# Attention with normalised queries and keys, then a SiLU feed-forward: a score unit moved in the late visits, two small writes moved to ScalarE, and another order and bank behind the last visit

## The chip, the cores and the metric

The kernel runs on one core of a Trainium2 chip. The metric is the device time of one execution in microseconds (us), and less is better. The engines are TensorE (PE in the profile; its weight loads are PEld), VectorE (DVE), ScalarE (ACT), GpSimd (POOL) and SyncE (SP, which issues most of the transfers). They run side by side, and each takes its own instructions in program order and waits for the others by semaphores.

## The reference

All inputs are 32-bit floats. Attention has 8 batches, 12 heads, 448 positions and 64 columns to a head; the feed-forward takes 3584 rows of 768 columns through 2048 hidden columns.

```python
def rmsnorm(x, g):
    rms = np.sqrt(np.mean(x * x, axis=-1, keepdims=True) + 1e-06)
    return x / rms * g
q_n, k_n = rmsnorm(q, g_q), rmsnorm(k, g_k)
scores = np.matmul(q_n, k_n.transpose(0, 1, 3, 2)) / np.sqrt(64)
attn = np.exp(scores - np.max(scores, axis=-1, keepdims=True))
attn = attn / (np.sum(attn, axis=-1, keepdims=True) + 1e-09)
x = np.matmul(attn, v).transpose(0, 2, 1, 3).reshape(8 * 448, 768)
h = x @ w_in
out = (h / (1 + np.exp(-h))) @ w_out
```

## The kernel before

**Visits.** The 96 heads are taken four at a time, as two pairs, in 24 *visits*: `visit(c)` for c from 0 to 23, and a last `visit(24)` that only finishes visit 23. Six visits are a group of two batches (`GROUP`). From visit 12 on (`LATE`) queries and keys are loaded in quarters and transposed by VectorE instead of TensorE. These are the late visits.

**What a visit does.** TensorE works in *units* of four 64 x 64 matmuls, which are written into one place of PSUM. A score unit (`scores`, matmuls on L709) fills one of two buffers named `sc`, and two exponentials on ScalarE (L714) read it into SBUF; the next unit but one in `sc` waits until they have. A value unit (`weigh`, L746) multiplies exponentials with rows of V, and adds into two banks, `av0` and `av1`, one for each pair of heads. A visit has seven score units and seven value units. They are written out by hand in one order, which is the order on TensorE. The last three value units of visit c - 1 (`weigh(c - 1, LEFT)`, `weigh(c - 1, LEFT - 1, 0)` and `weigh(c - 1, LEFT - 1, 1)`) lie in visit c. Then `divide(c - 1, sums)` on VectorE (L804, two instructions) reads both banks, multiplies by the reciprocal sums and writes columns of `x`. The first value unit of visit c, `weigh(c, 0, 1)`, writes the same two banks again: its first half waits for the divide of `av0`, its second half for that of `av1`.

**The one-column writes.** Where consecutive value units change the order of the array's halves, `turn` (L722) writes one unused column of bank `av1`, which waits for the matmuls into that bank and holds the next ones back. ScalarE or VectorE does it:

```python
turn(1, nc.scalar.copy if c <= GROUP else nc.vector.tensor_copy)
```

**Between visits.** `between(c)` makes the sums of exponentials and their reciprocals for visit c, prepares the next visits, and fills TensorE with the first layer of the feed-forward for the group before: products in Strassen's manner, seven for each block, from `x` and from `sums_x` (L882), in banks named `mm`. `scale(c + 2)` puts one small product in an `sc` buffer, which VectorE reads (L682). At the end of a group `sum_x` forms the differences of the columns of `x` that products 3 to 7 use: four VectorE instructions (L837) for each of three column indices. Index 0 is done in `between`, behind the last product that reads the old sums; indices 1 and 2 follow in the next visit, behind its divides.

**After the last visit.** When `visit(24)` is done, the six banks of `sc`, `av0` and `av1` go to a pool named `ps_alone`, and two more stay as `mm`. `bank` deals products out in turns of four, one to `mm` and three to `ps_alone`; `turns["next"]` says where it starts. The last group's first layer follows (L882), and then the second layer (L1226, and L1189 for most of it). Weight rounding and sums go beside it on VectorE, ScalarE and GpSimd.

Of the kernel before, what the change touches and what calls it, by code (L numbers as in the profile page):

```python
# [532 lines left out]
def bounded(  # L533
# [4 lines left out]
    HW, HF = z.NW // 2, z.NF // 2  # L538
# [5 lines left out]
    NC, loads, place, norm, spare, ones, first, squares = (  # L544
        own[name] for name in ("NC", "loads", "place", "norm", "spare", "ones", "first", "squares")
    )
    GROUP, LATE = z.NPAIR, z.LATE
# [55 lines left out]
    def weights(c, j):  # L603

        return other if j == 0 and c < GROUP and c % 2 else e[j]
# [4 lines left out]
    def x_of(c, i):  # L610
        b, cp = divmod(c, z.NPAIR // 2)
        return xT(b, 2 * cp + i)
# [87 lines left out]
    def scores(c, j, i=None):  # L700


        two = ps.tile([P, 2, BANK], F32, name="sc", bufs=2)
        for half in range(2):
            pair = half if j == LEFT else i
            keys = kT[:, ds((z.KA, z.KB)[0 if j == LEFT else i] + j * P, P)]
            for h in range(2):
                rows = ds(h * D, D)
                nc.tensor.matmul(  # L709
                    two[ds(half * D, D), h, 0:S], keys[rows, ts(half, D)], qT[rows, pair, :],  # L710
                    start=True, stop=True,
                )
        for h in range(2):
            nc.scalar.activation(  # L714
                eleft[:, h] if j == LEFT else weights(c, j)[:, i, h], two[:, h, 0:S], AF.Exp,
                scale=norm.column(c, i, h, j),
            )

    def turn(step, copy):

        if step != weighed["step"]:
            copy(banks[1][:, S : S + 1], minus_half)  # L722
# [78 lines left out]
    def divide(c, source):  # L801
        for i in range(2):
            x = x_of(c, i)
            nc.vector.tensor_tensor(  # L804
                out=x, in0=x if source is None else source[i], in1=r[i], op=ALU.mult
            )

    def normalise(c):


        def piece(name, i):
            t = scratch[i if c < GROUP + 2 else 0]
            source = raw_of(c) if c < GROUP else q_of(c)
            if name == "q":
                norm.squares_q(c, source, t, i)
            else:
                norm.squares_k(c, place["k0" if c >= LATE else f"k{c % 2}"], t, i)
            if name == "q" and c < GROUP:
                norm.root(c, name, i)
                norm.scale(c, source, q_of(c), i, nc.gpsimd)  # L820
                if i == 1 and c + 2 < GROUP:
                    load_q(c + 2)
            elif i == 1:
                norm.root(c, name)
                if name == "q":
                    for m in range(2):
                        norm.scale(c, source, q_of(c), m, nc.gpsimd)
                elif LATE <= c < NC - 1:
                    loads["k"](c + 1)

        if c >= NC:
            return []
        return [lambda a=a: piece(*a) for a in (("q", 0), ("q", 1), ("k", 0), ("k", 1))]
# [26 lines left out]
    turns = dict(next=0)  # L860
# [92 lines left out]
    def sum_x(group, c):  # L953
        right_sums(*quarters(group, c), *sums_of_x(c))
# [355 lines left out]
    def begin(work, columns, parts):  # L1310
        finish()
        filler.update(work=work, due=0.0, share=columns / parts)
# [31 lines left out]
    def finish():  # L1344
        run(filler["work"])
# [19 lines left out]
    def weights_in_visit(c):  # L1365
        for step in visits.get(c, ""):
            step_of[step]()
        if c in sums_visits:
            for step in range(4):
                sum_w_in(sums_visits[c], step)  # L1370

    def last_two(c):
        return [c // GROUP * 2 - 2, c // GROUP * 2 - 1]

    def visit(c):

        beside = normalise(c + 1) if c <= GROUP else []
        if c < NC:
            scores(c, 0, 0)
        run_all(beside[0:1])  # L1380
        if c > 0:
            weigh(c - 1, LEFT)
            weigh(c - 1, LEFT - 1, 0)
            turn(1, nc.scalar.copy if c <= GROUP else nc.vector.tensor_copy)
        if c < NC:
            scores(c, 0, 1)
        if c == 0:
            run_all(beside[1:2])
        if c > 0:
            weigh(c - 1, LEFT - 1, 1)  # L1390
            if c - 1 < EARLY:
                for i in range(2):
                    nc.vector.tensor_copy(x_of(c - 1, i), sums[i])
                run_all(beside[1:2])
                if inverting:
                    if c > 1:
                        divide(c - 2, None)
                    run_all(inverting)
                    inverting.clear()
            else:  # L1400
                divide(c - 1, sums)
                run_all(beside[1:2])
                if c < NC and c % GROUP == 0:
                    for i in range(0 if c == GROUP else 1, HW):
                        sum_x(last_two(c), i)
                weights_in_visit(c)
            if c + 1 < NC:
                loads["vrest"](c + 1)
        if c == NC:
            return  # L1410
        scores(c, 1, 0)
        scores(c, 1, 1)
        if c < GROUP:
            run_all(beside[2:3])
        weigh(c, 0, 1)
        scores(c, 2, 0)
        weigh(c, 1, 1)
        turn(0, nc.scalar.copy)
        if c < GROUP:
            run_all(beside[3:4])  # L1420
        scores(c, 2, 1)
        weigh(c, 0, 0)
        run_all(add(c, 1))
        weigh(c, 1, 0)
        scores(c, LEFT)
        if c + 1 < NC:
            loads["v"](c + 1)

    def run_all(work):
        for piece in work:  # L1430
            piece()

    def between(c):

        def transposes_and_sums():
            summing = sum_up(c)
            if c < GROUP:
                next(summing)
            if c < LATE - 1:
                transpose_k(c + 1)  # L1440
            reciprocals = next(summing)
            if LATE - 1 <= c < NC - 1:
                reciprocals += [lambda: flip(c + 1, "k"), gain]
            if GROUP // 2 <= c <= EARLY:
                divide(c - 1, None)
            return reciprocals

        if c < LATE - 1:
            transpose_q(c + 1)
        elif c < NC - 1:  # L1450
            flip(c + 1, "q")
        if c < GROUP // 2:
            inverting.extend(transposes_and_sums())
        elif c == GROUP - 1:
            run_all(transposes_and_sums())
        if c >= GROUP and c % GROUP == 0:
            fetched = range(AHEAD) if c == GROUP else ()
            columns = products - 2 * HW * S * len(fetched)
            work = halves_in(last_two(c), range(HF), plain_in, dict(begun), fetched)
            begin(work, columns, 2 * GROUP)  # L1460
            begun.clear()
        late = add(c, LEFT - 1) + add(c, LEFT) if c >= GROUP else []
        further = normalise(c + 2) if c >= GROUP - 1 else []
        fill(late + weights_in(c, 0) + further[2:])
        prompt = transposes_and_sums() if GROUP // 2 <= c != GROUP - 1 else []
        if c == GROUP // 2:
            begin(make_ahead([0, 1]), AHEAD * 2 * HW * S, GROUP - 1)
        if c >= LATE - 2:
            if c == LATE - 2:
                prompt.append(pair_up)  # L1470
            queries = prompt[3:] + [lambda: sum_squares(c + 2)]
            fill(weights_in(c, 1), prompt[:3] + [lambda: run_all(queries)])
        else:
            fill(weights_in(c, 1) + (further[:2] if c >= GROUP else []), prompt)
        if c % GROUP == GROUP - 1:
            finish()
            if c == GROUP - 1:
                begun[0] = fetch_ahead([0, 1], 0)
            else:
                sum_x([c // GROUP * 2, c // GROUP * 2 + 1], 0)  # L1480
        if c >= LATE - 2:
            scale(c + 2)
        if GROUP <= c < NC - 1:

            nc.scalar.activation(first, minus_half, AF.Exp)
        if c == NC - 1:
            while rounder.load():
                pass
# [12 lines left out]
    ps_alone = ctx.enter_context(  # L1501
        tc.tile_pool(name="ps_alone", bufs=6, space=bass.MemoryType.PSUM)
    )
    turns["next"] = 1
    group = [z.B - 2, z.B - 1]
    for i in (1, HW - 1):
        sum_x(group, i)
    for m in range(2):
        rows = [staged() for _ in range(2)]
# [215 lines left out]
```

## Time and profile before

| | |
|---|---|
| median of 3 runs | 1331.43 us (1331.42 to 1336.38) |
| profiled execution | 1333.6 us |
| its span in the profile | 1331.8 us |
| TensorE busy | 1301.7 us, 98% |
| VectorE busy | 942.2 us, 71% |
| ScalarE busy | 506.6 us, 38% |
| GpSimd busy | 363.8 us, 27% |
| late visits begin (first score) | visit 12 at 334.09 us, visit 18 at 538.39 us, visit 23 at 708.15 us |
| last visit and start of the last group's products | 742.7 to 748.3 us |

A span is the time from the first to the last instruction of the profiled execution. A row of a timeline gives start, length, engine, line, operation, what it writes and reads, and how many instructions of that kind were merged; in brackets how long the engine stood idle ahead of it, and what ended that. The end of a matmul in such rows is modelled, so the starts are the firmer numbers. A row of waits gives the engine and line that waited, who was waited for, the total in us, how often, and the longest.

### The profile page before, as it was taken

How to read it: one execution, taken by the hardware profiler on the slowest of the kernel's cores; microseconds unless marked ns; L12 is line 12 of the kernel's file. 1: busy time of each engine (PE TensorE's matmuls, PEld its weight loads, DVE VectorE, ACT ScalarE, POOL GpSimd, SP SyncE). 2: the span in 40 equal slices, each digit the busy share in tenths (PEclk: the TensorE clock that was granted, in tenths of full speed). 3: DMA queues.
4: the chain of work that ended last, by engine and by line, in shares of the span. 5: the costliest groups of instructions: out<-in, count | busy, mean ns of one | idle time of the engine just before them, and what ended most of it. 6: DMA issues, size and time to landing. Idle time of an engine off the chain costs nothing.

```text
span 1331.8 us, 19793 instructions
## 1 busy us (share of the span) xinstructions
PE 1301.7 (98%) x7189; PEld 833.1 (63%) x7189; DVE 942.2 (71%) x1623; ACT 506.6 (38%) x890; POOL 363.8 (27%) x229
## 2 busy tenths in 40 slices
PE   8998999999999999999999999999999999999998
PEld 4333444444444444444444455557999999999998
DVE  5787777785755555854554586688978787878785
ACT  7876556655454554455545244410001000001000
POOL 5765534344333433433330154410000000000000
PEclk9999999999999999999999999999999999999999
DMA  8564436333444444444321257522323232332311
GB/s 231 149 167 134 119 98 168 103 89 94 95 94 115 98 93 117 94 94 115 88 66 62 97 179 249 171 74 76 99 76 99 76 105 83 97 105 71 127 48 39
DMA packets 249487, 144.94 MB, mean 109 GB/s; under 512 B 184292, under 2 KB 233316, under 8 KB 249380
## 3 DMA queue, kind: packets, MB, share of 16 engines
q1 hardware_dynamic: 248816, 142.60, 38.0%
q8 instruction: 59, 0.97, 0.3%
q0 software_dynamic: 256, 0.79, 0.2%
q14 instruction: 48, 0.39, 0.1%
q10 hardware_dynamic: 308, 0.20, 0.1%
HBM read 93.98 MB, written 41.29 MB: 102 GB/s over the span
## 4 chain that ended last, share of the span: by engine, by line
PE 84%; DVE 7%; ACT 3%; issue 3%; DMA 2%; POOL 1%; SPq 0%; ACTq 0%; DVEq 0%; POOLq 0%
PE mm L882 26%; PE alone L1189 22%; PE av L746 8%; PE sc L709 7%; PE mm L1189 7%; PE alone L882 7%; PE alone L1226 2%; DVE work L760 1%; PE sc L780 1%; DVE work L789 1%; DVE sums_x L837 1%; DMA work<-work 1%; PE mm L1226 1%; PE sc L644 1%; PE sc L626 0%
## 5 line engine op out<-in xcount | busy, mean ns | idle before, releaser
L882 PE MATMUL mm<-x,W 128*128 128x448 f32 x636 | 256.7, 546 | 6.1 <-DVE parts L840 2.3
L714 ACT ACTIVATE work<-sc,rms 128x448 f32<-128x448 f32 x324 | 184.7, 633 | 81.0 <-PE sc L709 64.9
L882 PEld LDWEIGHTS mm<-x,W 128*128 128x128 f32 x636 | 116.7, 190 | 138.0 <-issue 109.0
L882 PE MATMUL mm<-sums_x,W 128*128 128x448 f32 x456 | 183.7, 543 | 1.6 <-DVE parts L840 1.6
L709 PE MATMUL sc<-work 64*64 64x448 f32 x1344 | 168.2, 549 | 2.6 <-ACT work L714 1.4
L746 PE MATMUL av<-work,rows 64*64 64x448 f32 x1296 | 156.6, 543 | 6.3 <-ACT av L722 1.8
L760 DVE TENSOR_TENSOR work<-work 128x896 f32<-128x896 f32 (+1 forms) x114 | 123.7, 1118 | 49.3 <-PE av L746 48.7
L493 POOL TENSOR_TENSOR rms<-rms,minus_half 128x14 f32<-128x14 f32 (+4 forms) x43 | 106.4, 2476 | 149.8 <-DVE rms L489 140.2
L882 PEld LDWEIGHTS mm<-sums_x,W 128*128 128x128 f32 x456 | 85.1, 190 | 90.7 <-issue 82.8
L520 POOL DMA_DIRECT2D out_dram<-x x2 | 1.3, 653 | 443.2 <-DVE x L840 443.2
L1189 PE MATMUL alone<-W,rows 128*128 128x192 f32 x608 | 113.0, 326 | 0.0
L746 PEld LDWEIGHTS av<-work,rows 64*64 64x64 f32 x1296 | 59.9, 133 | 78.0 <-issue 35.5
L709 PEld LDWEIGHTS sc<-work 64*64 64x64 f32 x1344 | 55.2, 134 | 73.8 <-ACT work L714 27.6
L1189 PEld LDWEIGHTS alone<-W,rows 128*128 128x128 f32 x608 | 101.2, 190 | 0.0
L902 POOL TENSOR_TENSOR parts<-parts,stage 128x448 f32<-128x448 f32 x31 | 42.0, 1356 | 148.7 <-DVE parts L840 148.4
L685 POOL TENSOR_TENSOR rms<-rms,minus_half 128x28 f32<-128x28 f32 x12 | 57.5, 4794 | 67.2 <-DVE rms L682 58.0
L1189 PE MATMUL alone<-W,work 128*128 128x192 f32 x382 | 72.2, 326 | 0.0
L1020 ACT ACTIVATE stage<-stage 128x896 f32<-128x896 f32 x63 | 57.3, 945 | 24.1 <-DVE stage L840 23.4
L465 DVE TENSOR_REDUCE rms<-rows 128x8 f32<-128x512 f32 (+2 forms) x56 | 35.9, 641 | 42.5 <-ACT rows L464 38.9
L1189 PEld LDWEIGHTS alone<-W,work 128*128 128x128 f32 x382 | 63.8, 190 | 0.0
L1199 ACT COPY rows<-alone 128x192 f32<-128x192 f32 x34 | 10.8, 317 | 137.8 <-PE alone L1189 79.0
L789 DVE RECIPROCAL work<-sc 128x224 f32<-128x224 f32 x36 | 55.7, 1548 | 5.2 <-PE sc L780 5.0
(244 smaller groups left out, 2115.4 us busy)
## 6 DMA issues: line engine op xcount, KB each, us to landing
hidden<-stage SPq DMA_DIRECT2D x63, 448.0 KB, 3.0
work<-hidden SPq DMA_DIRECT2D x21, 1024.0 KB, 5.0
rows<-in_moe_w_out_dram SPq DMA_DIRECT2D x32, 384.0 KB, 3.3
W<-in_moe_w_in_dram SPq DMA_DIRECT2D x22, 512.0 KB, 5.2
work<-work SPq DMA_DIRECT2D x144, 56.0 KB, 2.0
x<-hidden SPq DMA_DIRECT2D x7, 1024.0 KB, 6.1
rows<-in_q_dram SPq DMA_DIRECT2D x96, 56.0 KB, 2.2
rows<-in_k_dram SPq DMA_DIRECT2D x96, 56.0 KB, 2.3
```

The costliest lines, as they stand in the source:

```text
L493: nc.gpsimd.tensor_tensor(out=t, in0=t, in1=half, op=ALU.pow)
L685: nc.gpsimd.tensor_tensor(out=f, in0=f, in1=minus_half.to_broadcast([P, n]), op=ALU.pow)
L709: nc.tensor.matmul(two[ds(half * D, D), h, 0:S], keys[rows, ts(half, D)], qT[rows, pair, :], start=True, stop=True,)
L714: nc.scalar.activation(eleft[:, h] if j == LEFT else weights(c, j)[:, i, h], two[:, h, 0:S], AF.Exp, scale=norm.column(c, i, h, j),)
L746: nc.tensor.matmul(sums[i][ds(h * D, D), :], v, w, start=(j == 0 and step == 1), stop=(j == LEFT - 1 and step == 1),)
L760: nc.vector.tensor_tensor(out=total, in0=total, in1=more, op=ALU.add)
L789: nc.vector.reciprocal(out=r[0][:, rows], in_=t[:, rows])
L882: nc.tensor.matmul(t, self.left(name, s), self.right(name, s), start=s == ends[0], stop=s == ends[1])
L902: nc.gpsimd.tensor_tensor(out=u2, in0=u2, in1=p5, op=ALU.add)
L1020: nc.scalar.activation(t, t, AF.Silu)
L1189: nc.tensor.matmul(t, x[:, i], y, start=i == ORDER[0], stop=i == ORDER[-1])
L1226: nc.tensor.matmul(o, a[:, 2 * i + m, t], right_one(name, i)[:, m], start=n == 0, stop=n == len(steps) - 1,)
```

## The change

It has three parts. In visits 12 to 23 the third score unit, `scores(c, 1, 0)`, is issued ahead of `weigh(c - 1, LEFT - 1, 1)` instead of behind it. In visits 12 and 18 the one-column write of `turn(1, ...)` is made by ScalarE instead of VectorE (the condition also names visits 0 and 6, which ScalarE had already or which have no such write). After visit 23 the `sum_x` for column index 0 is no longer done in `between(23)`; all three indices follow the divides of `visit(24)`. And `turns["next"]` starts at 3 instead of 1, so that the first product after `visit(24)` takes an `mm` bank instead of one of `ps_alone`.

```diff
         if c > 0:
             weigh(c - 1, LEFT)
             weigh(c - 1, LEFT - 1, 0)
-            turn(1, nc.scalar.copy if c <= GROUP else nc.vector.tensor_copy)
+            turn(1, nc.scalar.copy if c <= GROUP or c in range(0, NC, GROUP) else nc.vector.tensor_copy)
         if c < NC:
             scores(c, 0, 1)
+        if LATE <= c < NC:
+            scores(c, 1, 0)
         if c == 0:
             run_all(beside[1:2])
         if c > 0:
...
         if c == NC:
             return
-        scores(c, 1, 0)
+        if c < LATE:
+            scores(c, 1, 0)
         scores(c, 1, 1)
...
             if c == GROUP - 1:
                 begun[0] = fetch_ahead([0, 1], 0)
-            else:
+            elif c < NC - 1:
                 sum_x([c // GROUP * 2, c // GROUP * 2 + 1], 0)
...
-    turns["next"] = 1
+    turns["next"] = 3
     group = [z.B - 2, z.B - 1]
-    for i in (1, HW - 1):
+    for i in range(HW):
         sum_x(group, i)
```

## The prediction

> **What bounds the kernel now.** The page's first section comes first: whose time is it?
>
> ```profile
> PE 1301.7 (98%) x7189; PEld 833.1 (63%) x7189; DVE 942.2 (71%) x1623; ACT 506.6 (38%) x890; POOL 363.8 (27%) x229
> ```
>
> TensorE works almost without a break, so an edit can win only what TensorE stands still, and loses whatever new stop it causes. The waits of TensorE say where it stands. First for 334 to 744 us, the twelve late visits (12 to 23) and what lies between them, then for 744 us to the end:
>
> ```profile
> PE sc L709 <- DVE rms L682: 1.2, 2, 0.6
> PE mm L882 <- DVE parts L840: 1.1, 3, 0.4
> PE sc L780 <- DVE work L760: 0.3, 1, 0.3
> ```
>
> ```profile
> PE av L746 <- DVE av L722: 1.5, 1, 1.5
> PE alone L882 <- DVE x L804: 1.4, 1, 1.4
> ```
>
> So 2.6 us of stops in 410 us of late stage, and 2.9 us in two stops at the last visit. No score unit waits for ScalarE, and no late product `av` waits for a divide long enough to be listed. That is a balance, though, and the timeline of visit 15 shows how much it can bear (start, length, engine, line; "x8" is one unit of four matmuls, each recorded twice; "x16" is two units):
>
> ```profile
> 438.92 0.93 PE L709 MATMUL sc<-work 64*64 64x448 f32 x8
> 439.67 0.93 PE L746 MATMUL av<-work,rows 64*64 64x448 f32 x8
> 440.42 1.72 PE L709 MATMUL sc<-work 64*64 64x448 f32 x16
> 441.96 0.93 PE L746 MATMUL av<-work,rows 64*64 64x448 f32 x8
> 442.71 0.56 PE L709 MATMUL sc<-work 64*64 64x448 f32 x4
> ```
>
> ```profile
> 440.67 1.16 DVE L804 TENSOR_TENSOR x<-av,work 128x448 f32<-128x448 f32 x2 [1.34 <-PE av L746]
> ```
>
> ```profile
> 437.66 1.16 ACT L714 ACTIVATE work<-sc,rms 128x448 f32<-128x448 f32 x2 [2.34 <-PE sc L709]
> 439.94 1.16 ACT L714 ACTIVATE work<-sc,rms 128x448 f32<-128x448 f32 x2 [1.12 <-PE sc L709]
> ```
>
> Starts lie 0.75 us apart: that is a unit's price on TensorE. The last unit of the visit before (`av` at 439.67) is read by two divides (L804) that start 1.00 us after it began, and end 1.62 and 2.16 us after it (one takes 0.62, the pair 1.16). The next visit's first `av` unit overwrites those banks. It starts 2.29 us after 439.67, with two score units in between, and reaches the second bank half a unit (0.375 us) later. So the divides are covered by two score units, with 2.29 + 0.375 - 2.16 = 0.5 us to spare at the tighter of the two: less than one unit.
>
> **What the Trainium skill says.** "Perfetto Trace Analysis", section "Tensor Engine Instruction (MATMUL, LD_WEIGHTS)": TensorE can only pull weight loads ahead, matmuls keep their order, while VectorE and ScalarE take theirs strictly in order; the end of a matmul in a trace is an estimate. The trace agrees as far as it goes: in visit 12 the writes stand behind L837 and L682 in program order (below); I therefore work from starts. "PSUM — Partial Sum Buffer", section "PSUM bank collisions raise a hardware error": TensorE writing a bank while VectorE reads it is an error that the chip does not hold off, so the wait for the divides can't be dropped; nothing in this trace shows a collision. "ScalarE: Activation LUTs", section "What ACT_TABLE_LOAD costs": about 1283 ns a load; here the loads ahead of the exponentials take 1.28 us.
>
> **The change part by part.** *Third score unit, visits 12 to 23.* No instruction is added. Four matmuls pass the four of the `av` unit of 439.67 on TensorE. Their two exponentials pass nothing on ScalarE, and no DMA is among them. On SP the loads of the V rows keep their order; those that wait for this `av` unit go 0.75 us later and are needed only a 34 us period later.
>
> What could it win? A visit takes 10.97 us from first score to first product (436.61 to 447.58); 14 units at 0.75 are 10.5 and the change of tile size at its end takes some 0.3 us. So at most about 0.15 us a visit.
>
> What it loses: `av` goes to 440.42, the divides to 441.42, ending at 442.04 and 442.58. The next `av` unit is due at about 441.95. A released TensorE starts 0.06 us after the release (at the last visit the write ends at 745.92 and TensorE starts at 745.98). As built, each half of the unit waits for its own divide: first half at 442.10, 0.375 us of work, second half not before 442.64, end at 443.02 against 442.71. Loss 0.31 us a visit, 3.7 us in twelve. From below it is bounded by 0 (both divides ready), from above by 0.68 (the whole unit waits for the second divide); I take 0.31.
>
> The third score also needs the buffer whose last reader is the first pair of exponentials. In visit 15 these end at 438.82, and the unit is due at 439.67: free. But where the switch from SiLU to Exp came late they don't:
>
> ```profile
> 335.75 1.28 ACT L1485 ACT_TABLE_LOAD   x1
> 337.15 2.27 ACT L714 ACTIVATE work<-sc,rms 128x448 f32<-128x448 f32 x4
> ```
>
> Visit 12: the first pair ends at 338.30, the unit is due at 337.16 + 0.75 = 337.91 and could start at 338.36: 0.45 us. The same sum gives 0.46 for visit 18 (pair from 541.45), 0.39 for visit 23 (from 710.39, due 711.21), 0.16 each for 13 (from 370.41, due 371.45) and 19 (from 574.65, due 575.69). Together 1.6 us, on top of the divides' loss, because `av` and divides move too. Late stage: +5.3 us.
>
> *The two one-column writes (visits 12 and 18).* Taken from VectorE (0.15 us each), they are put behind two exponentials on ScalarE. What stops TensorE there is a line ahead of them:
>
> ```profile
> 337.16 0.98 PE L709 MATMUL sc<-work 64*64 64x448 f32 x8 [0.58 <-DVE rms L682]
> ```
>
> ```profile
> 336.92 0.18 DVE L682 TENSOR_SCALAR rms<-sc 128x28 f32<-128x28 f32 x1
> 337.02 0.15 DVE L722 COPY av<-minus_half 128x1 f32<-128x1 f32 x1
> ```
>
> The second score waits for L682, itself behind four `sum_x` steps, and both stay. Gain 0. On ScalarE the write would end at about 338.30 + 0.17 = 338.47, before its reader `av` (now behind the third score, 339.11). Loss 0 too; without that cover it would be 338.53 - 337.96, 0.6 us.
>
> *The last visit.* In the chain and the timeline around 744 us:
>
> ```profile
> 745.77 0.15 DVE L722 COPY av<-minus_half 128x1 f32<-128x1 f32 x1
> 747.03 1.16 DVE L804 TENSOR_TENSOR x<-av,work 128x448 f32<-128x448 f32 x2 [1.11 <-PE av L746]
> ```
>
> ```profile
> 745.98 0.98 PE L746 MATMUL av<-work,rows 64*64 64x448 f32 x8 [1.54 <-DVE av L722]
> 748.33 4.75 PE L882 MATMUL alone<-x,W 128*128 128x448 f32 x12 [1.37 <-DVE x L804]
> ```
>
> With the four `sum_x` steps behind it, the write waits for TensorE alone. In visit 15 the corresponding write starts 0.25 us after the start of the next unit; here that is 744.21 + 0.25 = 744.46, so the last `av` unit starts at 744.68, 1.30 us earlier. The next product now writes an `mm` bank, whose readers have finished, not a bank that a divide reads: it starts at 744.68 + 0.75 + 0.3 = 745.73 instead of 748.33, another 1.30 us. Twelve `sum_x` steps now follow the divides (end 746.89): at 0.56 us each they end at 753.6. TensorE first has four products of 2.26 us that need none of them, to 754.8. Covered by 1.2 us. The second product, in an `alone` bank, comes at 748.0, after the divides. From here to about 1326 us no stop of TensorE is listed, so the 2.6 us reach the end. Bounds: 1.3 (only the write's wait goes) to 2.9 (both stops whole).
>
> *Sum.* 3.7 + 1.6 - 2.6 = +2.7 us: the profiled execution, 1333.6 us with a span of 1331.8, would become 1336.3. It stands 2.2 us above the median of 1331.43; against the median the forecast is **1334.1**.
>
> **The rivals.** *A, the cover suffices*: if the divides release sooner than their records say, the late visits lose nothing and the end's gain stands: 1328.8. For it: no wait for L804 is listed in the late visits. Against it: the spare 0.5 us is less than the 0.75 that the move takes away. Chance 0.12. *B, the whole unit waits*: if the first half too can go only after the second divide, a visit loses 442.64 - 441.96 = 0.68 us; 8.2 + 1.6 - 2.6 = +7.2, 1338.6. This is slower by more than 0.5%; it decides from a mean loss of (6.7 + 2.6) / 12 = 0.77 us a visit, exponentials included. For it: the restart after a broken stream may cost more than 0.06; against it: separate waits of the two halves. Chance 0.12. *C, the gain at the end fails*: the first product waits for some other reader or the sums come late: +5.3, 1336.7. Against it: the 1.2 us cover. Chance 0.12.
>
> **How the numbers follow.** 0.64 for my forecast, whose own range is 1331 to 1337. A range of 1330.0 to 1338.6 holds it, C and about half of B. No change is within 6.7 us (0.5%, about what a measurement of this kernel can tell from none): 0.84. Slower by more: 0.14, B and the spread of the runs (one of three lay 5 us up). Faster by more: 0.02; all stops in reach, 0.15 x 12 + 1.2 + 2.9, are 5.9 us.
>
> **What would show it.** Right: a new wait of `av` L746 for L804 in all late visits, 0.3 us each in two pieces; a wait of `sc` L709 for L714 of about 0.4 us in visits 12, 18 and 23; L682's wait unchanged; the two stops at 744 us reduced to about 0.25 us. Wrong: no wait for L804, or one above 0.6 us a visit, or a first `mm` product after 747 us.

## The result, and the profile after

The changed kernel takes 1338.6 us (median of 9 runs, 1337.1 to 1341.0), the kernel before 1332.1 us (9 runs beside it, 1331.4 to 1336.4). The ratio is 1.0037, with a 95% interval of 1.0025 to 1.0049: slower by 4.9 us (3.3 to 6.5), within 0.5%. The medians lie 6.5 us apart, at the upper end of that interval: six of the nine runs of the kernel before took 1331.4 to 1332.9 us, and three near 1336 us. The forecast was +2.7 us, 1334.1 us, with a range to 1338.6.

The profiled executions are 1338.6 and 1333.6 us long. Two stretches account for the difference. I read each visit's length from a timeline of TensorE: from its first score unit to the first product behind its last. Then I read the stretch from the last visit's first value unit to the first product of the last group.

| us | visit 12 | 15 | 18 | 23 | 12 to 23 together | last stretch |
|---|---|---|---|---|---|---|
| before | 11.83 | 10.97 | 11.77 | 11.02 | 133.4 | 5.63 |
| after | 12.85 | 11.51 | 12.75 | 11.97 | 141.8 | 2.93 |

So the late visits lose 8.4 us and the end wins 2.7. The other 0.7 us of the 5.0 lie outside: visit 12 begins 0.6 us earlier (333.47 instead of 334.09), ahead of every edit, and the rest after the first product is 0.1 us shorter. In the twelve traces of this case visit 12 begins between 331.57 and 334.09 us, though in all but one of them (`last_and_scale_first`) no edit comes before it: differences of this size between two executions say nothing of a change, so the lengths of the stretches are compared.

The page's first section shows that the same number of matmuls kept TensorE busy longer:

```profile
PE 1308.1 (98%) x7189; PEld 826.6 (62%) x7189; DVE 942.8 (71%) x1621; ACT 506.6 (38%) x892; POOL 363.3 (27%) x229
```

The waits of TensorE from 334 to 750 us, and from 750 us on:

```profile
PE sc L709 <- DVE rms L682: 1.2, 2, 0.6
PE mm L882 <- DVE parts L840: 1.1, 3, 0.4
PE mm L882 <- DVE stage L840: 0.5, 3, 0.2
PE sc L709 <- ACT av L722: 0.4, 2, 0.2
PE sc L780 <- DVE work L760: 0.3, 1, 0.3
PE sc L709 <- ACT work L714: 0.2, 1, 0.2
```

```profile
PE av L746 <- DVE av L722: 0.3, 1, 0.3
```

The stop of 1.5 us for the write became 0.3, the one of 1.4 us for the divide is gone, L682's two stops are unchanged. The new short waits for L840 cost nothing that can be seen: between the visits the two traces differ by 0.05 us in all. Yet a wait of the value unit for the divides (L804), which I had named as the sign of the loss, is in neither list. It shows only in the weight loads and in the order of the matmuls. Visit 15 again, TensorE, then VectorE, then the weight loads:

```profile
440.70 1.68 PE L709 MATMUL sc<-work 64*64 64x448 f32 x16
442.20 0.93 PE L746 MATMUL av<-work,rows 64*64 64x448 f32 x8
442.96 0.96 PE L709 MATMUL sc<-work 64*64 64x448 f32 x8
443.88 1.12 PE L746 MATMUL av<-work,rows 64*64 64x448 f32 x6
444.69 0.54 PE L709 MATMUL sc<-work 64*64 64x448 f32 x2
444.84 0.54 PE L746 MATMUL av<-work,rows 64*64 64x448 f32 x2
445.06 0.70 PE L709 MATMUL sc<-work 64*64 64x448 f32 x4
```

```profile
443.20 1.15 DVE L804 TENSOR_TENSOR x<-av,work 128x448 f32<-128x448 f32 x2 [2.09 <-PE av L746]
```

```profile
443.88 0.20 PEld L746 LDWEIGHTS av<-work,rows 64*64 64x64 f32 x4 [0.74 <-DVE x L804]
444.41 0.14 PEld L746 LDWEIGHTS av<-work,rows 64*64 64x64 f32 x2 [0.33 <-DVE x L804]
```

The unit of 442.20 is the one that was pushed back; the divides that read it start 1.00 us later, as before. The first half of the next value unit starts at 443.88, 0.06 us after the first divide's end, and its second half at 444.41, behind the second divide. Before the change both halves started together: in visit 15 of the kernel before the unit's four matmuls begin between 441.956 and 441.976 us, and the second record of each follows 0.376 us later. Now the unit's eight records stand as "x6" and "x2", with two of the next score unit between them: one half of the array has gone on while the other is behind, so TensorE counts as busy, and no wait is listed.

The last visit:

```profile
752.33 0.16 DVE L722 COPY av<-minus_half 128x1 f32<-128x1 f32 x1 [0.92 <-PE av L746]
753.60 1.15 DVE L804 TENSOR_TENSOR x<-av,work 128x448 f32<-128x448 f32 x2 [1.10 <-PE av L746]
```

```profile
752.55 0.98 PE L746 MATMUL av<-work,rows 64*64 64x448 f32 x8 [0.28 <-DVE av L722]
753.46 2.52 PE L882 MATMUL mm<-x,W 128*128 128x448 f32 x6
```

The write now waits for TensorE alone, and the first product starts while the divides still run.

### The profile page after: what moved, and what is told of

It reads as the page before. It is cut to its first block, busy times and chain, and to the rows that moved or that the text cites. A ratio compares the mean times of both kernels' runs of the same rounds, so it can differ in the third digit from the quotient of the medians.

```text
span 1336.8 us, 19781 instructions
## 1 busy us (share of the span) xinstructions
PE 1308.1 (98%) x7189; PEld 826.6 (62%) x7189; DVE 942.8 (71%) x1621; ACT 506.6 (38%) x892; POOL 363.3 (27%) x229
## 4 chain that ended last, share of the span: by engine, by line
PE 82%; DVE 6%; ACT 5%; issue 3%; DMA 3%; POOL 1%; SPq 1%; ACTq 0%; DVEq 0%; POOLq 0%
PE mm L882 24%; PE alone L1189 22%; PE av L746 8%; PE mm L1189 7%; PE sc L709 7%; PE alone L882 7%; PE alone L1226 2%; DVE work L789 1%; DVE work L760 1%; PE sc L780 1%; DMA work<-work 1%; PE mm L1226 1%; ACT stage L1020 1%; ACT work L714 1%; PE sc L644 1%
## 5 line engine op out<-in xcount | busy, mean ns | idle before, releaser
L882 PE MATMUL mm<-x,W 128*128 128x448 f32 x612 | 247.2, 547 | 6.6 <-DVE stage L840 2.7
L714 ACT ACTIVATE work<-sc,rms 128x448 f32<-128x448 f32 x324 | 185.1, 633 | 89.3 <-PE sc L709 73.2
L882 PEld LDWEIGHTS mm<-x,W 128*128 128x128 f32 x612 | 112.1, 190 | 134.4 <-issue 104.9
L882 PE MATMUL mm<-sums_x,W 128*128 128x448 f32 x480 | 193.4, 543 | 1.6 <-DVE parts L840 1.6
L709 PE MATMUL sc<-work 64*64 64x448 f32 x1344 | 174.0, 546 | 3.1 <-ACT work L714 1.5
L746 PE MATMUL av<-work,rows 64*64 64x448 f32 x1296 | 162.3, 543 | 4.3 <-ACT av L722 1.8
L882 PEld LDWEIGHTS mm<-sums_x,W 128*128 128x128 f32 x480 | 89.6, 190 | 95.2 <-issue 86.9
L746 PEld LDWEIGHTS av<-work,rows 64*64 64x64 f32 x1296 | 55.3, 132 | 89.2 <-issue 42.8
L882 PE MATMUL alone<-x,W 128*128 128x448 f32 x156 | 61.1, 539 | 0.0
```

Of the source, the lines that this page charges most:

```text
L709: nc.tensor.matmul(two[ds(half * D, D), h, 0:S], keys[rows, ts(half, D)], qT[rows, pair, :], start=True, stop=True,)
L714: nc.scalar.activation(eleft[:, h] if j == LEFT else weights(c, j)[:, i, h], two[:, h, 0:S], AF.Exp, scale=norm.column(c, i, h, j),)
L746: nc.tensor.matmul(sums[i][ds(h * D, D), :], v, w, start=(j == 0 and step == 1), stop=(j == LEFT - 1 and step == 1),)
L882: nc.tensor.matmul(t, self.left(name, s), self.right(name, s), start=s == ends[0], stop=s == ends[1])
```

## The experiments

Theory 1: the late visits lose because the divides are covered by one score unit instead of two, and because the two halves of a value unit run side by side, so that the second half's whole lateness counts. The rivals blame the ScalarE writes, ScalarE's exponentials or the order of matmuls itself. The last part gains by itself. Diffs are against the kernel before where nothing else is said.

**The moved score unit alone** (`scores_only`). Its diff holds the change's lines on `scores(c, 1, 0)`.

```diff
+        if LATE <= c < NC:
+            scores(c, 1, 0)
...
-        scores(c, 1, 0)
+        if c < LATE:
+            scores(c, 1, 0)
```

> The kernel before with the moved third score unit alone (visits 12 to 23). Theory 1 (the late visits lose because the divides keep one score unit of cover instead of two, and the two halves of the value unit run side by side on the array, so that the second half's whole lateness counts): ordinary late visits 11.5 us from first score to first product instead of 10.97, and all twelve together about 8 us longer; the run is slower by about 8 us. Theory 2 (the moved unit is harmless, and the loss comes with the two ScalarE writes or with what follows the last visit): less than 1 us.

Ratio 1.0064 (1.0051 to 1.0077), +8.5 us (6.8 to 10.3). Visit 15 takes 11.51 us, the twelve visits 141.9 us, as in the changed kernel (141.8). So this part brings the whole loss in the late visits, and theory 2 falls.

**The part behind the last visit alone** (`last_only`).

```diff
-            else:
+            elif c < NC - 1:
                 sum_x([c // GROUP * 2, c // GROUP * 2 + 1], 0)
...
-    turns["next"] = 1
+    turns["next"] = 3
-    for i in (1, HW - 1):
+    for i in range(HW):
```

> The kernel before with the part behind the last visit alone (x sums behind the divides, first product in an mm bank). Theory 1: the stretch from the last visit's first value unit to the first product goes from 5.6 us to 2.9 us, and since TensorE doesn't stop after that, the run is faster by about 2.7 us. Rival: the gain is eaten later, by sums that come late or by VectorE work that has slipped; then the stretch is shorter and the run is not faster.

Ratio 0.9972 (0.9960 to 0.9984), 3.7 us faster (2.1 to 5.3). The last stretch is 2.93 us, the twelve visits 133.5 us. The gain reaches the end.

**Its two halves** (`bank_only`, `sums_only`). One has only the new start of `turns`, the other only the moved sums.

> The kernel before with the other bank for the first product after the last visit alone; the sums of x stay ahead of the divides. Theory 1: TensorE's stop of 1.5 us for the one-column write stays, the one of 1.4 us for the divide goes: the stretch from the last visit's first value unit to the first product is 4.3 us instead of 5.6. Rival (the first product waits for the divide's results or for the sums, not for the bank): 5.6 us stay.

> The kernel before with the sums of x behind the divides of the last visit alone; the first product still takes a bank that a divide reads. Theory 1: the stop for the write falls from 1.5 to 0.3 us, the stop for the divide stays at 1.4: a stretch of 4.3 to 4.4 us. Rival: the divide was late only because of the sums; then both go and the stretch is 2.9 us.

The stretches are 4.19 and 4.37 us. TensorE's rows, first with the bank alone, then with the sums alone:

```profile
745.37 0.98 PE L746 MATMUL av<-work,rows 64*64 64x448 f32 x8 [1.54 <-DVE av L722]
746.28 2.15 PE L882 MATMUL mm<-x,W 128*128 128x448 f32 x5
```

```profile
742.20 0.98 PE L746 MATMUL av<-work,rows 64*64 64x448 f32 x8 [0.28 <-DVE av L722]
744.55 1.74 PE L882 MATMUL alone<-x,W 128*128 128x448 f32 x4 [1.37 <-DVE x L804]
```

Each edit removes one stop and leaves the other: 1.44 and 1.26 us, together the 2.70 of the whole part.

**The two writes alone** (`writes_only`).

```diff
-            turn(1, nc.scalar.copy if c <= GROUP else nc.vector.tensor_copy)
+            turn(1, nc.scalar.copy if c <= GROUP or c in range(0, NC, GROUP) else nc.vector.tensor_copy)
```

> The kernel before with the two one-column writes on ScalarE alone (visits 12 and 18), without the moved score unit. Theory 1: TensorE's stop ahead of the second score stays at 0.6 us, because VectorE's L682 ends it; and the write now stands behind two exponentials that start late, so that the value unit behind the second score waits some 0.6 us in each of the two visits: 12.4 us instead of 11.8, the run slower by about 1.2 us. Rival (the write was what held TensorE up): visits 12 and 18 get shorter by about 0.6 us each.

Visits 12 and 18 take 12.33 and 12.27 us, 0.50 more each. The ratio, 0.9997 (0.9989 to 1.0005), does not show this 1.0 us, and the upper end of its interval, 0.7 us, falls short of it. So the loss is read from the two visits of one trace and is not confirmed by the runs. In visit 12:

```profile
336.35 0.98 PE L709 MATMUL sc<-work 64*64 64x448 f32 x8 [0.58 <-DVE rms L682]
337.60 0.98 PE L746 MATMUL av<-work,rows 64*64 64x448 f32 x8 [0.27 <-ACT av L722]
```

L682 ends the first stop, as before; the write on ScalarE makes a second one. In the changed kernel the moved score unit covers it: visit 12 takes 12.85 us there and 12.86 with the moved unit alone.

**The changed kernel with short divides** (`after_short_divides`, diff against the changed kernel).

```diff
+            n = S // 4 if LATE <= c + 1 < NC else S
             nc.vector.tensor_tensor(
-                out=x, in0=x if source is None else source[i], in1=r[i], op=ALU.mult
+                out=x[:, 0:n], in0=(x if source is None else source[i])[:, 0:n],
+                in1=r[i][:, 0:n], op=ALU.mult,
             )
```

> The changed kernel with the divides of the late visits cut to a quarter of their columns (112 of 448; the other columns of x are left undivided and unwritten). Theory 1: the pair of divides ends about 0.7 us earlier, so ordinary late visits fall from 11.5 us to 10.8 to 11.0; the late stage as a whole falls by 6 to 8 us. Rival (the loss comes from ScalarE's buffer wait or from the order of the matmuls itself): visits stay at 11.3 us or more.

Visit 15 takes 10.83 us, the twelve 133.8 us. The order of the change is now 0.14 us faster in an ordinary visit than the order before (10.97). Visits 12, 18 and 23 stay longer than before, at 12.18, 12.08 and 11.35 us, and three waits of the score unit for ScalarE, 0.2 us each, stay in the list of waits: that is ScalarE's part.

**The kernel before with short divides** (`before_short_divides`), the same edit there.

> The kernel before with both divides of the late visits cut to a quarter of their columns (the other columns of x are left undivided and unwritten). Theory 1: there the divides are covered by two score units, so ordinary late visits stay at 10.9 to 11.0 us. Rival (the divides already held TensorE up in the kernel before): they fall to 10.8 us or less.

Visit 15 takes 10.97 us, the twelve 133.4 us, unchanged: with two score units of cover the divides cost nothing.

**Only the first divide short** (`after_first_divide_short`): the edit in the changed kernel for `i == 0` alone.

> The changed kernel with only the first of the two divides of a late visit cut to a quarter of its columns (the rest of that half of x is left undivided and unwritten). The second divide then ends 1.8 us instead of 2.2 us after the start of the value unit that it reads, and the first one in good time. Theory 1 (the two halves of a value unit run side by side, so that the second is due together with the first, 1.5 us after that start): the second half comes some 0.35 us late, and ordinary late visits take 11.1 to 11.25 us. The prediction's sum (the halves run one after the other, the second due 0.375 us after the first): nothing is late, and the visits take 10.8 to 10.9 us, as with both divides cut.

Visit 15 takes 11.18 us, the twelve 138.3 us. The first half of the value unit starts at 443.12. The second half waits for the second divide and starts at 443.46, 0.34 us late, still in the row "x6"; two matmuls of the next score unit start before it is done:

```profile
443.12 0.93 PE L746 MATMUL av<-work,rows 64*64 64x448 f32 x6
443.87 0.55 PE L709 MATMUL sc<-work 64*64 64x448 f32 x2
443.88 0.54 PE L746 MATMUL av<-work,rows 64*64 64x448 f32 x2
```

The visit is 0.35 us longer than with both divides short (10.83). So the halves run side by side, and the prediction's sum, which had them one after the other, falls.

**The first value unit one place back** (`after_value_back`, against the changed kernel).

```diff
+        if c >= LATE:
+            scores(c, 2, 0)
         weigh(c, 0, 1)
-        scores(c, 2, 0)
+        if c < LATE:
+            scores(c, 2, 0)
```

> The changed kernel with one more exchange in the late visits: the fifth score unit goes ahead of the visit's first value unit, so that the divides have two score units of cover again. Theory 1 (cover of the divides): the second half of the value unit no longer comes late; what is left is the fifth score's wait for the exponentials of the third, 0.3 us or less, so ordinary late visits go from 11.5 us to 10.9 to 11.2. Rival (the order of score and value units itself costs, or ScalarE can't follow): 11.5 us or more stay.

Visit 15 takes 11.01 us, the twelve 134.1 us; the ratio to the kernel before, with the gain at the end in it, is 0.9984 (0.9977 to 0.9991). With two score units between the value units again, the loss is gone, although the third score stands where the change put it.

**A faster version** (`last_and_scale_first`): the last part, and the scaling ahead of the sums at the ends of groups.

```diff
+        if c >= LATE - 2:
+            scale(c + 2)
         if c % GROUP == GROUP - 1 and GROUP - 1 < c < NC - 1:
             sum_x([c // GROUP * 2, c // GROUP * 2 + 1], 0)
-        if c >= LATE - 2:
-            scale(c + 2)
```

> The kernel before with the part behind the last visit, and with the small product and L682 of the scaling issued ahead of the four sums of x at the ends of groups (visits 12 and 18); no moved score unit, no write on ScalarE. Theory 1 (L682, behind the sums on VectorE, is what stops TensorE ahead of the second score): the stop of 0.6 us goes, a wait of at most 0.2 us for the one-column write takes its place, visits 12 and 18 fall from 11.8 us to 11.0 to 11.3, and the run is faster than the kernel before by 2.7 + 1.2 = 3.9 us. Rival (another wait stands right behind it): 11.6 us or more, and the run is faster by 2.7 us.

Ratio 0.9970 (0.9959 to 0.9982), 4.0 us faster than the kernel before. L682's stop is gone, but visits 12 and 18 only fall to 11.59 and 11.54 us:

```profile
334.51 0.93 PE L709 MATMUL sc<-work 64*64 64x448 f32 x8
335.34 0.98 PE L746 MATMUL av<-work,rows 64*64 64x448 f32 x8
336.45 2.03 PE L709 MATMUL sc<-work 64*64 64x448 f32 x16
```

The third score unit starts 1.11 us after the value unit instead of 0.75: a wait that L682's had hidden takes half or more of the expected gain, and the visits end close to the 11.6 us of the rival. From its place it is the wait for the first pair of exponentials; I made no run to prove that. The gain over the last part alone is 0.5 us in the trace and can't be told apart in the runs.

## Why the prediction was right, and where it was off

The forecast of no change beyond 0.5% held. The mechanism held too, but one of its terms was too small, and that the range still holds the median is luck: 1338.6 us is the very end of the range and the figure of rival B, and the forecast counted from a median of three runs, 1331.43 us, from which the median after lies 7.2 us away. Step by step:

- **The divides lose their cover: right. The size: off.** The failed step is "first half at 442.10, 0.375 us of work, second half not before 442.64, end at 443.02 against 442.71. Loss 0.31 us a visit". It let the halves follow one another: the 0.375 us that it gave to the second half are the time to the second record of each matmul, as the starts in the kernel before show. The spare time that it put at 0.5 us was by the same slip 2.29 - 2.16 - 0.06 = 0.07 us. The halves start together, and the second half's lateness counts in full: 0.68 us, which the prediction had as its upper bound. Against that stand 0.14 us that the new order gives back (10.83 against 10.97 us with short divides), perhaps by the earlier exponentials; no run shows by what. 0.68 - 0.14 = 0.54, and visit 15 lost 0.54. Twelve times that is 6.5 us instead of 3.7.
- **What could be won in a visit, at most 0.15 us: right.** The short divides show 0.14.
- **Late exponentials in visits 12, 13, 18, 19 and 23: right.** Summed at 1.6 us, they are what is left, 8.4 - 6.5 = 1.9 us, and all but 0.1 us of it lies in these five visits. In visit 12 the third score was due at 336.54 + 0.75 = 337.29 and came at 337.72, 0.43 us late, where the sum had 0.45 (its lines stand below this list).
- **The two writes: right**, nothing in the changed kernel, and a loss without the cover: 0.50 us a visit in the trace, estimated at 0.6.
- **The last visit: right**, 2.70 us for 2.6, in two halves of 1.26 and 1.44 for 1.30 each. The sums behind the divides were covered.
- **The signs.** The prediction named two signs of being wrong, no wait for L804 or one above 0.6 us a visit, and read by the list of waits the first of them came: TensorE's waits show none, since the other half of the array went on working; only the weight loads name it. The lateness itself, 0.68 us, is above the second limit. The waits of `sc` for ScalarE came in visits 12, 18 and 23, but are listed with 0.2 us each instead of 0.4. The trace also seems to depart from the reading that I took from the Trainium skill ("Perfetto Trace Analysis", section "Tensor Engine Instruction (MATMUL, LD_WEIGHTS)"), that only weight loads are pulled ahead. `scores` issues its four matmuls to the two halves in turn, yet two of them start at 444.69 and the other two at 445.22. If each pair belongs to one half, a matmul passed one that stands ahead of it; the records don't name the half, so this stays open.
- **The rivals.** A (no loss) and C (no gain at the end) are excluded; A's figure also left out the 1.6 us of the exponentials, which don't depend on the divides. B had the right size of lateness, 0.68, and with it the measured median, but the mean loss, 8.4 / 12 = 0.70 us a visit, is under the 0.77 that was to decide for it, and its mechanism is wrong: the first half does not wait for the second divide, it starts at 443.88, 0.06 us after the first.

The second and the third score unit of visit 12 in the changed kernel:

```profile
336.54 0.98 PE L709 MATMUL sc<-work 64*64 64x448 f32 x8 [0.58 <-DVE rms L682]
337.72 0.98 PE L709 MATMUL sc<-work 64*64 64x448 f32 x8 [0.20 <-ACT av L722]
```

The row shows 0.20 us of the 0.43, since idle time counts from the modelled end of the unit before. It names the write that stands behind the first pair of exponentials on ScalarE. That pair ended at 337.67, 0.05 us ahead of the third score, and with the moved unit alone, where ScalarE makes no such write, the same 0.20 us are put down to the exponentials (L714).

The sum with the measured terms is 6.5 + 1.9 - 2.7 = +5.7 us, less the 0.7 us outside the stretches: the 5.0 us between the profiled executions.

## What to carry to other kernels

When a unit of work is moved, count the units that stay between a result's last write and the next write of its bank: a move by one place takes a whole unit (here 0.75 us) from that cover, and what the readers then lack is lost in every visit (here 0.68 us). Where two halves of the array had waits of their own, the later half set the cost, and it hid from the list of waits, so compare the lengths of whole stages. A part that gains and one that loses can sit in one change: here the last two edits alone are worth keeping.

## What the runs showed of the hardware that was not expected

In two of the four traces that still have both stops at the last visit (`scores_only` and `before_short_divides`, not in the kernel before or `writes_only`), the matmuls behind the stops ran at half speed for 3.41 us. With the moved score unit alone, the row of the first two products and two windows of 3 us from 753 us on (the number ahead of the DMA share is the granted clock):

```profile
754.50 6.44 PE L882 MATMUL alone<-x,W 128*128 128x448 f32 x12 [1.37 <-DVE x L804]
```

```profile
753.00:756.00 3.00, 1.63 (x7) 0.94 (x4) 2.77 (x6) 0.00 (x0) 0.00 (x0) 0.82 0.96 345
756.00:759.00 3.00, 3.00 (x6) 1.33 (x6) 2.84 (x6) 0.23 (x1) 0.00 (x0) 0.61 0.12 46
```

The same twelve records take 4.75 us in the kernel before; the slow ones cost 6.44 - 4.75 = 1.7 us. With the moved score unit alone the trace's clock record stands at one half from 754.95 to 758.36 us. The Trainium skill ("TensorE: Matmul & The Clock Gate", section "What's actually happening") describes such a gate, with windows of about 3.4 us that run freely, and the trace agrees in length (3.41 us) and in the factor of two (a clock of 0.5). The page puts the slow clock behind at least one idle window of that length; here two stops of 1.54 and 1.37 us with some work between them were followed by it, in two of four traces; that they bring it about is not shown. None of the traces that lack one or both of the stops shows it at that place. The kernel before also has one such window, from 132.29 to 135.70 us, behind a single stop of 1.8 us; the changed kernel stops for 1.6 us there and has none. Slow windows of this kind in some runs of the kernel before may be why the last part alone measured 3.7 us in the runs where its trace explains 2.7, but the interval holds both, and so does the spread of the executions ahead of visit 12; I made no run for it.
